# The same last stretch for one gated attention and Fourier kernel, with three reorderings in its first tenth: the third tokens' transposes behind scores, one copy behind the second keys' cast, the weights' exponential one tile later

## The chip, the cores and the metric

The kernel runs on one core of a Trainium2 chip. The core has five engines, each with its own in-order queue: PE (TensorE, matrix products, with weight loads shown as PEld), DVE (VectorE), ACT (ScalarE), POOL (GpSimd) and SP (SyncE, which here only issues DMAs; ACT and POOL issue some too). Engines meet through semaphores. The metric is the device time of one execution in microseconds; runs are compared by their medians, and the traces come from one profiled execution each.

## The reference

```python
def _A_ref(x, wqkv, wo):                      # x: 1 x 2048 x 448, 16 heads of 28
    qkv = (x @ wqkv).reshape(B, S, 3, H, Dh).transpose(2, 0, 3, 1, 4)
    q, k, v = qkv[0], qkv[1], qkv[2]
    scores = jnp.einsum("bhqd,bhkd->bhqk", q, k) * Dh ** -0.5
    p = softmax(scores, axis=-1)
    o = jnp.einsum("bhqk,bhkd->bhqd", p, v)
    return o.transpose(0, 2, 1, 3).reshape(B, S, D) @ wo

def _B_ref(x, w_r, w_i):
    X = rfft2(x.astype(float32), axes=(-2, -1)) * (w_r + 1j * w_i)
    return irfft2(X, s=(S, D), axes=(-2, -1)).astype(bfloat16)

g = sigmoid((x * gate_w).sum(-1, keepdims=True))
return g * _A_ref(x, A_wqkv, A_wo) + (1 - g) * _B_ref(x, B_w_r, B_w_i)
```

Only `A_x` is used as x in both halves. Inputs and the output are bfloat16.

## The kernel before

**Attention.** The 16 heads go in four groups T of four heads, and the 2048 queries in four chunks of 512, so there are 16 chunks c = 4T + qc. For one chunk there are 16 key blocks i of 128 keys and 4 heads h: 64 pieces of 128 keys by 512 queries. `score` (L824) makes one piece on PE with 32 rows of the array, so products of four heads can run side by side. Most pieces are gathered into tiles of three or two pieces in turn (`next_tile`, L1156): `scores` (L1001) writes the tile to a bank of PSUM, `exp` (L1067) runs ACT's exponential over it (L1077) into a tile Pt, and `pv` (L981) multiplies Pt by the values `vsb` into the accumulator psPV (L998). A part of the pieces is taken off ACT: `claim` hands a key block to `pack_step` (L837), which casts the scores on DVE (L843, tile Pd), and `chain` (L849) makes the exponential of it on DVE by seven steps. The values carry a column of ones (of weights `ek` for the first group), so psPV holds the softmax's sums too.

**Everything else** is cut into units of a few phases, each a few PE instructions followed by DVE work: transposes of x (`turn_unit`), projections of queries and keys (`first_unit` for the first group, `qk_unit` later), values (`v0_unit`, `v_unit`), the gate, the Fourier half as products with cosine and sine matrices (`f1_unit`, `a_unit`, `b_unit`, `i_unit`, `z_unit`), and the output tiles (`out_unit`, `base_unit`). They use two background banks of PSUM, bg0 and bg1, and in the beginning the accumulator's bank as a third (named pv).

**The order is written out when the program is built.** `stream` (L1330) walks over the tiles k with modelled clocks: `tp` for PE, `tv` for DVE, `ta` for ACT. For each tile it emits the exponential k, a few value products (`do_pv`, L1399), as many unit phases as fit (`pick`, `step` L1222), dummy products on a zero tile `warm` that keep PE busy (`zero`, `one_zero`, `until` at L1290 and L1296, `zeros` at L1034), and then the scores of tile k + 2, which use the PSUM bank that exponential k has read. Emission order is the order in each engine's queue; what it waits for follows from the tiles it touches. `bank_free` is the modelled time at which each of the three banks can be written again, and the bank that is free first takes the next unit.

**The head.** `head` (L299) brings the first 256-token pieces through by hand. Then the units in FIRSTS come: T1.2, T2.0, k0.1, T2.2, T3.0, k0.2, T3.2, k0.3, q0.1, ek0, W0 to W3. T2.0 and T2.2 are the two halves of the transposes of the third 512 tokens (448 columns of x in four pieces), each eight PE transposes (L296) and one DVE copy into xT (L447). k0.1 is the second 512 keys of the first group: two products and two more (L288), a DVE cast to `qraw` (L609) and its square `sqh` (L610), a product that adds the norms (L614), and the cast into kT (L618). The xtok tokens come by DMA from SP (L211, three loads of 512 tokens). The tiles' scores need kT of the block they read: the seventh tile is the first to use keys of k0.1. `ek_unit` finds each key's norm relative to the smallest one; its `weights` runs ACT's exponential (L488) and a DVE copy (L489) into vsb.

**The tail.** The last chunk's last four key blocks are cut in query parts of 256, 128 and 128 (`PARTS`, `split`), so that the end of one part is worked on while the next is computed. `pv_part` (L1456) multiplies the values of a part (L993), and when a part is complete DVE turns it (`over`: transposition L1555, reciprocal L1556, times gate L1557), scales it (`scaled`, L1560; on POOL for the first part, on DVE for the others) and turns it back into oT (`back`, L1565). `tail` (L1485) then makes output tiles 12 to 15. Each is what the earlier heads and the Fourier half gave (`base`, float32 in SBUF) plus the product of oT with Wo (`last_values`, L1543). For tiles 13 and 15 PE adds the base by a float32 product with the unit matrix (`sums`, L1538); for 14 DVE adds it (`add_base`, L820); for 12 ACT copies the product out (L1527) and POOL adds (L1528). The stores go out on SP's queue (12, 13, 14) and ACT's (15). Tile 12 and 13 use the first part, 14 the second, 15 the third.

Of the kernel before, what the change touches and what calls it, by code (L numbers as in the profile page):

```python
# [11 lines left out]
BF16 = mybir.dt.bfloat16  # L12
F16 = mybir.dt.float16
F32 = mybir.dt.float32
# [148 lines left out]
class Kernel:  # L163
# [286 lines left out]
    def ek_unit(self):  # L450
# [36 lines left out]
        def weights():  # L487
            nc.scalar.activation(out=ek[:], in_=ek[:], func=ACT.Exp, scale=-SCALE)  # L488
            nc.vector.tensor_copy(out=self.vsb[:, :, 0:4, DH], in_=ek[:].rearrange("p (t s) -> p t s", s=4))  # L489
            self.dve(0.25, at=self.ta + 0.4)  # L490
            self.marks["ek1"] = self.tp
# [489 lines left out]
    def pv(self, c, i, first, last):  # L981
        T = c // 4
        pcs = self.pieces.pop((c, i))
        self.packs -= self.pack_t[(c, i)] is not None
        if not isinstance(i, int):
            q0, w = PARTS[i[1]]
            n = len(i[2:])

            pairs = [(j, h) for j in range(n) for h in range(4)]
            if i[1] == len(PARTS) - 1:  # L990
                pairs.sort(key=lambda jh: jh[1])
            for j, h in pairs:
                self.nc.tensor.matmul(self.psPV[32 * h:32 * h + 32, q0:q0 + w], lhsT=self.vsb[:, i[2 + j], 4 * T + h, :],  # L993
                                      rhs=pcs[h][:, w * j:w * j + w], start=False, stop=True,
                                      tile_position=(0, 32 * h), skip_group_check=True)
# [71 lines left out]
    def exp(self, k):  # L1067
# [9 lines left out]
        self.nc.scalar.activation(out=Pt[:, 0:n, :], in_=ps[:, 0:n, :], func=ACT.Exp, scale=SCALE)  # L1077
        for e, (c, i, h) in enumerate(self.tiles[k]):
# [143 lines left out]
    def step(self, u, b, limit):  # L1222
# [15 lines left out]
        pe(ps)  # L1238
# [3 lines left out]
        if ve is not None:  # L1242
            self.dve(vcost, at=self.tp + PV)
            ve(ps)
            self.bank_free[b] = self.tv + VP
# [6 lines left out]
        return True  # L1252

# [76 lines left out]
    def stream(self):  # L1330
# [5 lines left out]
        self.ended, self.ot, self.held = False, None, None  # L1336
# [21 lines left out]
        while self.ring:  # L1358
# [34 lines left out]
            self.scores(k + 2, end)  # L1393
            self.fill_v(end - 0.2)
# [4 lines left out]
    def do_pv(self, k, left, most, limit=0.0):  # L1399
        done = 0  # L1400
        waited = False
        while done < most and self.pv_c < NC:
# [28 lines left out]
            if c == NC - 1 and (len(left[c]) == 1 or not isinstance(cand, int) and waited):  # L1431
                break
# [52 lines left out]
    def tail(self):  # L1485
# [8 lines left out]
        for i in sorted(left[c], key=lambda i: (i,) if isinstance(i, int) else i):  # L1494
            if len(left[c]) == 1:
# [15 lines left out]
                for e in (0, 1):  # L1511
                    self.last_values(pf[e], e, e == 0)
# [5 lines left out]
            else:  # L1518
                self.pv_part(i)
        for n in (3, 2) if self.N % 2 == 0 else (2, 3):  # L1520
            pf.append(self.psp.tile([P, n, QW], F32, name=f"ps{n}", tag=f"ps{n}", bufs=1)[:, 0])
# [12 lines left out]
        nc.scalar.dma_start(out=self.outv[:, 15, :], in_=fin[2][:, 0:D])  # L1534
# [87 lines left out]
```

## Time and profile before

| | us |
|---|---|
| median of 3 runs | 426.28 (426.26 to 426.36) |
| the profiled execution | 427.39 |
| its span, first to last instruction | 425.60 |
| granted TensorE clock, mean | 1.000 |
| ACT tile exponentials (L1077), main group | 385.3 in 339, mean 1.300 |
| PE score products (L829) | 143.7 in 926 |
| DVE casts Pd (L843) | 88.6 in 130 |
| PE value products (L998) | 79.9 in 818 |
| dummy products on PE (L1296 and L1034) | 40.1 in 124 and 35.3 in 92 |

A row of the timeline reads: start, time, engine, line, operation, output tile and inputs, shapes, how many; in brackets the idle time of the engine just before it and what ended that. Rows that follow each other with the same line are merged. A row of the waits names the waiting engine, line and tile, what it waited for, and the total, the number of times and the longest. Matmul ends are modelled, and a few records of matmuls are missing.

The chain that ended last gives PE 35% of the span, ACT 34%, DVE 19%, issue (time in which an engine waited for nothing that the profile shows) 9% and DMA 2%.

### The profile page before, as it was taken

How to read it: one execution, taken by the hardware profiler on the slowest of the kernel's cores; microseconds unless marked ns; L12 is line 12 of the kernel's file. 1: busy time of each engine (PE TensorE's matmuls, PEld its weight loads, DVE VectorE, ACT ScalarE, POOL GpSimd, SP SyncE). 2: the span in 40 equal slices, each digit the busy share in tenths (PEclk: the TensorE clock that was granted, in tenths of full speed). 3: DMA queues.
4: the chain of work that ended last, by engine and by line, in shares of the span. 5: the costliest groups of instructions: out<-in, count | busy, mean ns of one | idle time of the engine just before them, and what ended most of it. 6: DMA issues, size and time to landing. Idle time of an engine off the chain costs nothing.

```text
span 425.6 us, 8292 instructions
## 1 busy us (share of the span) xinstructions
PE 406.7 (96%) x3178; PEld 146.1 (34%) x3197; DVE 394.7 (93%) x650; ACT 411.9 (97%) x370; POOL 50.8 (12%) x57
## 2 busy tenths in 40 slices
PE   8999999999999999999999999999999999999995
PEld 5444233333333333333333333333343333333332
DVE  6569989999989999999999999999999999999994
ACT  4899999999999999999999999999999999999994
POOL 6000002020110111011220100202001011110101
PEclk9999999999999999999999999999999999999999
DMA  8900310422302153375664446536453305222132
GB/s 231 183 6 2 8 27 7 113 51 52 77 13 42 31 96 62 74 166 99 144 158 99 108 103 124 103 70 109 109 148 78 76 2 101 56 70 65 32 62 67
DMA packets 32404, 34.30 MB, mean 81 GB/s; under 512 B 14988, under 2 KB 25228, under 8 KB 32332
## 3 DMA queue, kind: packets, MB, share of 16 engines
q1 hardware_dynamic: 28012, 20.21, 20.7%
q0 software_dynamic: 3600, 13.11, 16.9%
q8 instruction: 25, 0.41, 0.4%
q10 hardware_dynamic: 752, 0.44, 0.4%
q14 instruction: 15, 0.12, 0.1%
HBM read 14.85 MB, written 1.95 MB: 39 GB/s over the span
## 4 chain that ended last, share of the span: by engine, by line
PE 35%; ACT 34%; DVE 19%; issue 9%; DMA 2%; SPq 0%; ACTq 0%; DVEq 0%
ACT Pt L1077 29%; PE psPV L998 7%; PE ps L829 6%; DVE Pd L843 4%; PE bg L829 3%; PE psPV L1296 3%; PE bg L288 3%; ACT early L1077 2%; PE bg L1034 2%; DMA xtok<-in_A_x_dram 2%; DVE pa L887 2%; DVE Pd L864 1%; DVE n L861 1%; DVE pa L873 1%; PE bg L673 1%
## 5 line engine op out<-in xcount | busy, mean ns | idle before, releaser
L1077 ACT ACTIVATE Pt<-ps 128x1024 bf16<-128x1024 f32 (+1 forms) x339 | 385.3, 1300 | 0.9 <-PE ps L829 0.4
L829 PE MATMUL ps<-qT,kT 32*128 32x512 bf16 (+2 forms) x926 | 143.7, 375 | 3.7 <-ACT Pt L1077 2.0
L843 DVE TENSOR_SCALAR Pd<-bg 128x512 uint16<-128x512 f32 x130 | 88.6, 682 | 4.8 <-PE ps L829 3.4
L998 PE MATMUL psPV<-Pt,vsb 128*32 128x512 bf16 x818 | 79.9, 388 | 0.0
L829 PEld LDWEIGHTS <-kT 32*128 32x128 bf16 x1056 | 45.7, 91 | 93.9 <-issue 88.9
L829 PE MATMUL bg<-qT,kT 32*128 32x512 bf16 x130 | 49.8, 383 | 0.8 <-DVE Pd L843 0.3
L890 POOL DMA_DIRECT2D Pd<-pa x25 | 24.0, 962 | 218.4 <-PE ps L829 110.6
L887 DVE TENSOR_TENSOR pa<-pa,n 128x2048 uint16<-128x2048 f16 (+2 forms) x33 | 40.4, 1225 | 0.6
L873 DVE TENSOR_TENSOR pa<-pa,n 128x2048 f16<-128x2048 f16 (+1 forms) x33 | 40.3, 1222 | 0.3
L998 PEld LDWEIGHTS <-vsb 128*32 128x32 bf16 x1008 | 23.1, 93 | 50.9 <-issue 50.2
L1296 PE MATMUL psPV<-warm 128*128 128x512 bf16 x124 | 40.1, 385 | 0.0
L1034 PE MATMUL bg<-warm 32*128 32x512 bf16 x92 | 35.3, 383 | 1.8 <-DVE Pd L843 1.4
L975 POOL TENSOR_TENSOR oT<-o,rep 128x512 bf16<-128x512 f32 x13 | 16.4, 1264 | 134.8 <-DVE oT L974 67.0
L288 PE MATMUL bg<-xT,Wg 128*128 128x512 bf16 (+1 forms) x93 | 28.1, 381 | 1.1
L864 DVE TENSOR_SCALAR Pd<-Pd 128x2048 uint16<-128x2048 uint16 (+1 forms) x33 | 24.0, 726 | 0.4
L861 DVE TENSOR_SCALAR n<-Pd 128x2048 uint16<-128x2048 uint16 (+1 forms) x33 | 22.6, 684 | 0.4
L876 DVE TENSOR_SCALAR pa<-pa 128x2048 f16<-128x2048 f16 (+1 forms) x33 | 22.8, 691 | 0.1
L869 DVE TENSOR_SCALAR pa<-n 128x2048 f16<-128x2048 uint16 (+1 forms) x33 | 22.2, 674 | 0.0
L684 DVE CAST U<-bg 128x450 bf16<-128x450 f32 x32 | 19.9, 621 | 2.0 <-PE bg L696 1.2
L1034 PEld LDWEIGHTS <-warm 32*128 32x128 bf16 x92 | 8.3, 91 | 29.0 <-issue 28.2
L1077 ACT ACTIVATE early<-ps 128x1024 bf16<-128x1024 f32 (+1 forms) x13 | 15.2, 1227 | 2.3 <-PE ps L829 2.3
L782 PE MATMUL bg<-Binv,VT 128*128 128x448 bf16 x64 | 16.5, 355 | 0.4 <-DVE fin L792 0.3
(190 smaller groups left out, 431.9 us busy)
## 6 DMA issues: line engine op xcount, KB each, us to landing
Pd<-pa POOLq DMA_DIRECT2D x25, 512.0 KB, 5.0
rep<-rD SPq DMA_DIRECT2D x52, 64.0 KB
CR<-cRB SPq DMA_DIRECT2D x8, 256.0 KB
UT<-U SPq DMA_DIRECT2D x16, 112.5 KB
VT<-U SPq DMA_DIRECT2D x16, 112.5 KB
CR<-cCS SPq DMA_DIRECT2D x8, 192.0 KB
xtok<-in_A_x_dram SPq DMA_DIRECT2D x3, 448.0 KB
out_dram<-fin SPq DMA_DIRECT2D x12, 112.0 KB
```

What stands on the lines that cost most here:

```text
L288: self.nc.tensor.matmul(ps[:], lhsT=self.Wg[T, q][0:k, c, :], rhs=self.xT[0:k, c, 512 * b:512 * b + 512], start=(c == 0), stop=(c == 3))
L829: self.nc.tensor.matmul(out[:, w * j:w * j + w], lhsT=self.kT[T][32 * h:32 * h + 32, 128 * i:128 * i + 128], rhs=self.qT[T][32 * h:32 * h ...
L843: nc.vector.tensor_scalar(out=pk["t"][:, h, :], in0=ps[:], scalar1=SCALE * LOG2E * 512.0, scalar2=127.0 * 512.0, op0=ALU.mult, op1=ALU.add)
L861: v.tensor_scalar(out=st["n"], in0=t, scalar1=511, scalar2=None, op0=ALU.bitwise_and)
L864: v.tensor_scalar(out=t, in0=t, scalar1=127 << 9, scalar2=2, op0=ALU.bitwise_and, op1=ALU.logical_shift_right)
L873: v.tensor_tensor(out=st["a"], in0=st["a"], in1=st["n"], op=ALU.mult)
L887: v.tensor_tensor(out=q, in0=st["a"], in1=st["n"], op=ALU.mult)
L890: nc.gpsimd.dma_start(out=t, in_=q, accum_op=ALU.add)
L998: self.nc.tensor.matmul(self.psPV[32 * h:32 * h + 32, :], lhsT=self.vsb[:, i, 4 * T + h, :], rhs=pcs[h], start=first, stop=last, tile_posi ...
L1034: self.nc.tensor.matmul(ps[:], lhsT=self.warm[sl], rhs=with_free(self.warm[sl], [[0, 4], [1, P]]), start=True, stop=True, tile_position=(3 ...
L1077: self.nc.scalar.activation(out=Pt[:, 0:n, :], in_=ps[:, 0:n, :], func=ACT.Exp, scale=SCALE)
L1296: self.nc.tensor.matmul(self.psPV[:], lhsT=self.warm[:], rhs=with_free(self.warm[:], [[0, 4], [1, P]]), start=False, stop=False, skip_grou ...
```

## The change

Three orders change in the first tenth. The transposes of T2.0 are held back (`behind`) and emitted after the scores that follow; the bank is taken as free 1.0 us later by the planner, and one dummy product in front of the next scores is no longer emitted. The DVE copy of T3.0 is held back (`held`) while unit k0.1 is open, and emitted behind k0.1's cast into kT; the two background banks exchange names from there on. The exponential of the weights and its copy (`next_exp`) are emitted behind the next tile's exponential instead of ahead of it.

In the last stretch, a part of the last chunk may be taken by `do_pv` although it was waited for, as long as the modelled time is not over the limit: eight of the sixteen 256-column value products move ahead of twelve score products. In the last part the products are ordered by key block over the heads 0 to 2, then the four of head 3 (which alone need the last exponential), instead of head by head. The products with Wo for tiles 12 and 13 move behind the last part's values. Tile 12 is added by DVE as tile 14 is, last of all, and its store comes last on SP's queue; ACT's copy and POOL's add for it are gone. No other order changes on any engine.

```diff
@@ ek_unit
         def weights():
-            nc.scalar.activation(out=ek[:], in_=ek[:], func=ACT.Exp, scale=-SCALE)
-            nc.vector.tensor_copy(out=self.vsb[:, :, 0:4, DH], in_=ek[:].rearrange("p (t s) -> p t s", s=4))
+            def emit():
+                nc.scalar.activation(out=ek[:], in_=ek[:], func=ACT.Exp, scale=-SCALE)
+                nc.vector.tensor_copy(out=self.vsb[:, :, 0:4, DH], in_=ek[:].rearrange("p (t s) -> p t s", s=4))
+
+            self.next_exp = emit
@@ pv
-            pairs = [(j, h) for j in range(n) for h in range(4)]
-            if i[1] == len(PARTS) - 1:
-                pairs.sort(key=lambda jh: jh[1])
-            for j, h in pairs:
-                self.nc.tensor.matmul(self.psPV[32 * h:32 * h + 32, q0:q0 + w], ...
+            def heads(hs):
+                for j, b in enumerate(i[2:]):
+                    for h in hs:
+                        self.nc.tensor.matmul(self.psPV[32 * h:32 * h + 32, q0:q0 + w], ...
+            if i[1] < len(PARTS) - 1:
+                heads(range(4))
+            else:
+                assert len(self.tiles[self.N - 1]) == 1
+                heads(range(3))
+                heads((3,))
@@ exp
         self.nc.scalar.activation(out=Pt[:, 0:n, :], in_=ps[:, 0:n, :], func=ACT.Exp, scale=SCALE)
+        if self.next_exp:
+            self.next_exp()
+            self.next_exp = None
@@ step
-        pe(ps)
+        more = 0.0
+        if u.name == "T2.0":
+            self.behind.append(lambda ve=ve: (pe(ps), ve(ps)))
+            ve, more = self.later, 1.0
+        else:
+            pe(ps)
...
-            ve(ps)
-            self.bank_free[b] = self.tv + VP
+            if u.name == "T3.0" and any(x.name == "k0.1" for x, _ in self.open.values()):
+                self.held = lambda: ve(ps)
+            else:
+                ve(ps)
+            self.bank_free[b] = self.tv + VP + more
+            if u.name == "k0.1" and not u.phases and self.held:
+                self.held()
+                self.held = None
+                self.bank_free[0:2] = self.bank_free[1] + 0.6, self.bank_free[0]
...
+    def later(self, ps):
+        pass
@@ stream
             self.scores(k + 2, end)
+            while self.behind:
+                self.behind.pop()()
@@ do_pv
-            if c == NC - 1 and (len(left[c]) == 1 or not isinstance(cand, int) and waited):
+            if c == NC - 1 and (len(left[c]) == 1 or not isinstance(cand, int) and waited and self.tp > limit):
@@ tail
                 self.sums(pf[1], 1)
-                for e in (0, 1):
-                    self.last_values(pf[e], e, e == 0)
...
                 self.pv_part(i)
+        for e in (0, 1):
+            self.last_values(pf[e], e, e == 0)
...
-        fin = [self.rot3.tile([P, F2], BF16, name="X1") for _ in range(3)]
-        half = self.rot2.tile([P, QW], F32, name="o32")
-        nc.scalar.copy(out=half[:, 0:D], in_=pf[0][:, 0:D])
-        nc.gpsimd.tensor_tensor(out=fin[0][:, 0:D], in0=half[:, 0:D], in1=self.base[12], op=ALU.add)
-        nc.sync.dma_start(out=self.outv[:, 12, :], in_=fin[0][:, 0:D])
-        nc.scalar.copy(out=fin[1][:, 0:D], in_=pf[1][:, 0:D])
-        nc.sync.dma_start(out=self.outv[:, 13, :], in_=fin[1][:, 0:D])
+        fin = [self.rot3.tile([P, F2], BF16, name="X1") for _ in range(2)]
+        nc.scalar.copy(out=fin[0][:, 0:D], in_=pf[1][:, 0:D])
+        nc.sync.dma_start(out=self.outv[:, 13, :], in_=fin[0][:, 0:D])
         self.add_base(pf[3], 14, nc.sync)
-        nc.scalar.copy(out=fin[2][:, 0:D], in_=pf[2][:, 0:D])
-        nc.scalar.dma_start(out=self.outv[:, 15, :], in_=fin[2][:, 0:D])
+        nc.scalar.copy(out=fin[1][:, 0:D], in_=pf[2][:, 0:D])
+        nc.scalar.dma_start(out=self.outv[:, 15, :], in_=fin[1][:, 0:D])
+        self.add_base(pf[0], 12, nc.sync)
```

More of the change, by code (lines that the diff above doesn't have):

```diff
@@ L986, in pv @@
             q0, w = PARTS[i[1]]
-            n = len(i[2:])
-            pairs = [(j, h) for j in range(n) for h in range(4)]
-            if i[1] == len(PARTS) - 1:
-                pairs.sort(key=lambda jh: jh[1])
-            for j, h in pairs:
-                self.nc.tensor.matmul(self.psPV[32 * h:32 * h + 32, q0:q0 + w], lhsT=self.vsb[:, i[2 + j], 4 * T + h, :],
-                                      rhs=pcs[h][:, w * j:w * j + w], start=False, stop=True,
-                                      tile_position=(0, 32 * h), skip_group_check=True)
+            def heads(hs):
+                for j, b in enumerate(i[2:]):
+                    for h in hs:
+                        self.nc.tensor.matmul(self.psPV[32 * h:32 * h + 32, q0:q0 + w], lhsT=self.vsb[:, b, 4 * T + h, :],
+                                              rhs=pcs[h][:, w * j:w * j + w], start=False, stop=True,
+                                              tile_position=(0, 32 * h), skip_group_check=True)
+            if i[1] < len(PARTS) - 1:
[4 more added lines that the diff above has]
+                heads((3,))
             return
@@ L1335, in stream @@
         self.dummies = self.owed = 0
-        self.ended, self.ot, self.held = False, None, None
+        self.ended, self.ot, self.held, self.next_exp = False, None, None, None
+        self.behind = []
         self.pv_c, self.pv_free, self.pv_open = 0, 0.0, False
```

## The prediction

> **What bounds the kernel now.** I read the page first: which engine is full.
>
> ```profile
> PE 406.7 (96%) x3178; PEld 146.1 (34%) x3197; DVE 394.7 (93%) x650; ACT 411.9 (97%) x370; POOL 50.8 (12%) x57
> ```
>
> ACT, which runs the exponentials, is busy 411.9 of 425.6 us. Second, who makes ACT wait, asked for 60 to 430 us (total, times, longest), and ACT's own rows in the head:
>
> ```profile
> ACT Pt L1077 <- PE ps L829: 0.4, 2, 0.2
> ```
>
> ```profile
> 9.05 2.36 ACT L1077 ACTIVATE early<-ps 128x1536 bf16<-128x1536 f32 x2 [0.71 <-PE ps L829]
> 12.55 4.65 ACT L1077 ACTIVATE early<-ps 128x1536 bf16<-128x1536 f32 x4 [1.14 <-PE ps L829]
> 17.67 1.45 ACT L1077 ACTIVATE early<-ps 128x1536 bf16<-128x1536 f32 x1 [0.47 <-PE ps L829]
> ```
>
> The reader is to see: from 17.67 us to the last exponential ACT loses 0.4 us to waits. What ACT gains before 17.67 therefore travels to the end, and what the tail gains behind the last exponential (418.30) comes on top. Two places matter. The first is PE in the head:
>
> ```profile
> 9.14 0.65 PE L296 MATMUL pv<-ident,xtok 128*112 128x128 bf16 x8
> 10.63 0.65 PE L296 MATMUL bg<-ident,xtok 128*112 128x128 bf16 x8 [0.83 <-DMA xtok<-in_A_x_dram]
> 11.77 0.38 PE L1290 MATMUL pv<-warm 128*128 128x512 bf16 x1
> 12.08 0.39 PE L829 MATMUL ps<-qT,kT 32*128 32x512 bf16 x3
> 17.24 0.39 PE L829 MATMUL ps<-qT,kT 32*128 32x512 bf16 x2 [0.21 <-DVE kT L618]
> ```
>
> The transposes of the third tokens stand ahead of the third tile's scores (12.08) and wait for a load until 10.63; ACT, free at 11.41, waits until 12.55. At 17.24 the seventh tile's scores wait for the second keys. Why these are late stands in DVE's rows, where the last copy is the one waited for:
>
> ```profile
> 14.96 0.42 DVE L610 TENSOR_TENSOR sqh<-qraw 128x512 bf16<-128x512 bf16 x1
> 15.30 0.68 DVE L447 COPY xT<-pv 112x1024 bf16<-112x1024 bf16 x1
> 15.90 0.68 DVE L447 COPY xT<-bg 112x1024 bf16<-112x1024 bf16 x1
> 16.50 0.68 DVE L618 CAST kT<-bg 128x512 bf16<-128x512 f32 x1
> ```
>
> Third, the tail, where the chain of waits runs PE, DVE, PE, DVE, PE, ACT:
>
> ```profile
> 415.95 0.62 PE L993 MATMUL psPV<-Pt,vsb 128*32 128x256 bf16 x16
> 417.13 0.41 PE L993 MATMUL psPV<-Pt,vsb 128*32 128x128 bf16 x16 [0.23 <-DVE ot L1555]
> 418.75 0.55 PE L1543 MATMUL bg<-Wo,oT 128*128 128x448 bf16 x2 [0.26 <-DVE oT L1565]
> 419.23 0.44 PE L993 MATMUL psPV<-Pt,vsb 128*32 128x128 bf16 x16
> 421.68 0.36 PE L1543 MATMUL ps<-Wo,oT 128*128 128x448 bf16 x1 [0.88 <-DVE oT L1565]
> ```
>
> ```profile
> 418.15 0.17 DVE L1557 TENSOR_TENSOR i<-i,g 128x4 f32<-128x4 f32 x1
> 419.76 0.32 DVE L1555 STREAM_TRANSPOSE ot<-psPV 128x128 f32<-128x128 f32 x1 [0.55 <-PE psPV L993]
> 420.33 0.62 DVE L1557 TENSOR_TENSOR i<-i,g 128x4 f32<-128x4 f32 x1
> ```
>
> ```profile
> 422.64 0.35 ACTq L1534 DMA_DIRECT2D out_dram<-X  x1
> ```
>
> The last values (419.23) stand in PE's queue behind two output products (418.75) that wait for DVE, though their last exponential ended at 418.30. The same small product on DVE (L1557) takes 0.17 once and 0.62 the second time; POOL's add for output tile 12 runs from 419.80 to 420.93, just over it.
>
> **The head, step by step.** New order on PE: transposes T1.2, three dummies, scores of the third tile, T2.0. The third dummy writes the bank that T1.2's copy leaves at 9.83+0.69 = 10.52, so it starts at 10.57. From that dummy to the exponential the trace has 12.55-11.77 = 0.78, hence 11.35; ACT is free at 11.31 (exponentials overlap by 0.10). Gain so far 1.20.
>
> PE goes on, with the trace's own distances: T2.0 0.32 behind the scores, 11.21 (the load landed at 10.59: 0.6 of cover; k0.1 and the fourth scores queue behind that wait); eight transposes 0.45; two products of k0.1 at 11.66 and 11.88; the fourth tile's scores 12.18 (the dummy ahead of them is gone); k0.1's other two 12.50 and 12.72; T2.2 12.95; the fifth tile's scores 13.49, whose exponential can start at 13.49+0.39+0.08 = 13.96. ACT would be free at 13.62 (11.35 plus 1.35 plus 0.92 for the two exponentials): a new wait of 0.34.
>
> DVE: the cast qraw starts 0.57 behind the last k0.1 product (as 14.16 to 13.59), 13.29; sqh 14.09 to 14.51; T2.2's copy 14.43 to 15.11. Now kT is next, not T3.0's copy: its norm product can run at 14.57 and is done by 14.99, so kT takes 15.03 to 15.71; the seventh scores start at 15.77, their exponential could at 16.23, and ACT comes free at 16.26. Trace: 17.67. **Gain in the head 1.41 us.** Check by idle times: 1.24 and 0.57 go (counted with the overlap), 0.40 are new.
>
> T3.0's copy follows, 15.63 to 16.31; the next instruction that needs it is PE's dummy at 16.61: hidden with 0.25 to spare. The keys k0.2 behind it are first needed by the thirteenth tile, over 3 us later than they are made. T2.0's copy on DVE runs at 11.9, where DVE stood idle for 2.15.
>
> The exponential of the weights (0.26 on ACT) is only exchanged with a tile's: ACT's sum stays. Its copy (0.31) falls behind a Pd cast that had 0.58 of idle ahead of it, and pushes the raw query by 0.31, of which 0.21 of idle ahead of W0's product takes most; the last 0.1 lies on DVE, which is not the bound. Without that cover it would cost 0.31 once. Price 0.
>
> Bounds for the head. Above: all idle goes, 1.81. Below: the landing records of the trace show fifteen of the sixteen parts of the third tokens' load in by 7.99 and one at 10.59; if that straggler comes early in an execution without profiler, the kernel before loses less. T2.0 would then run at 9.78, everything up to 12.55 would be 0.85 earlier, kT would end at 16.33 and the exponential start at 16.82: gain 0.56. I take 1.41, what this trace says.
>
> **The middle.** Between tail and head every engine's order is the same; the two background banks only change names. Nothing there hangs on absolute time but the initial loads, the last issued by 15.84. I carry the 1.41 through; bounds 0 and all of it.
>
> **The tail, in the old clock.** Eight of the sixteen 256-column value products move ahead of the twelve score products at 415.60, which wait for an exponential until 415.55; they take 0.22 of the 0.35 from 415.25 to 415.60, and the dummy there runs beside the scores. So the first part ends 0.22 earlier, and with it DVE's first transposition (416.41), the second part's values (416.91), and the float32 sums behind them (417.25 to 418.27). The last part's first twelve products start at 418.20, the four that need the last exponential (418.30) follow at 418.40 and are done by about 418.7. DVE is still at the second part until 419.00, so the last transposition starts at 419.03, not 419.76: 0.73.
> Then, 0.03 apart, 0.32, 0.18, 0.17 (POOL's add is gone, so L1557 costs 0.17, not 0.62: 0.46), 0.29, 0.31: oT complete at 420.40. PE meanwhile ran the two products for tiles 12 and 13 (0.58), the sums (0.86 to the next start), tile 14's product (to 420.35); tile 15's starts at 420.45, not 421.68; ACT copies at 420.86 and issues the store at 421.42, not 422.64. But tile 12 is new on DVE: add for 14 from 420.40, add for 12 (0.58 each, as L820) to 421.48, store 421.51. On SP's queue that store goes from first to last, so 13 and 14 no longer stand behind it. Both land 1.7 after issue as before (421.51 against 422.64): **gain in the tail 1.13 us.**
> Bounds: above 1.2 (tile 15's own path); below 0.6, if the last values end 0.4 later than I think, which tile 15's product then feels in full since PE has only 0.1 of slack there, and the stores of 12 and 15 get 0.15 in each other's way.
>
> The 0.46 rests on one overlap; POOL's product at 417.60 to 418.21 also touches an L1557 (418.15) and costs it nothing. If POOL is not the cause, the tail gives 0.67, within these bounds; I take 1.13, as the long row is the only one that lies under a POOL row from its start.
> [...]
>
> **Sum.** 1.41 + 1.13 = 2.54. Span 425.60 to 423.06; the profiled execution took 427.39, 1.79 more than its span, so it would take 424.85. The median of the runs shown, 426.28, is 1.11 below that execution; I take the same difference off it: **423.8 us**. Own range of this case 423.2 to 424.4.
>
> **Rivals.**
> 1. *The head pays little*: the straggler is the profiler's (for it: the profiled execution is 1.11 longer than the median; against it: nothing ties the 1.11 to that place), or DVE at 93% takes the shift up in mid-stream. 0.56 + 1.13: 424.6; nothing at all: 425.1.
> 2. *The tail gives it back*: the products now stacked behind the last values (0.58, 0.86, 0.35) or the second add decide. With no gain there 426.28-1.41 = 424.9. Against it: 1.1 us of lateness is needed, the stack's own slack is 0.1 but its rows are all measured.
> 3. *It does not do what it says*: kT is held up elsewhere (its norm product, its qraw) and the tail's POOL add was harmless: under 0.85 in all, 425.5 to 426.3.
> 4. *Slower: PE's clock drops in the head.* One dummy product is taken out and the order of full and partial ones changes. The windows row (busy times of PE, weight loads, DVE, ACT, POOL, then the granted clock) speaks against it:
>
> ```profile
> 9.00:10.60 1.60, 0.79 (x11) 0.51 (x8) 1.43 (x3) 1.55 (x2) 0.00 (x0) 1.00 1.11 139
> ```
>
> PE idles half of this stretch and the clock stays 1.00, there and in the stretches behind it; the new order idles less. If it fell to half: PE is busy 6.62 of the 7.10 us from 10.60 to 17.70, so each such microsecond costs 0.93. From 2.7 us on it eats the 2.54; 4 us of it give 427.5.
> [...]
>
> **How the numbers follow.** Forecast 0.62, rival 1 0.17, rival 2 0.10, rival 3 0.06, rival 4 0.05. A measurement of this kernel can tell about 0.2%, 0.85 us, from no change. Forecast, 1 and 2 are all faster by more: 0.89; rival 3 is within: 0.06; rival 4 slower: 0.05. Range: 2.54 with the lower bounds 0.56 and 0.6 gives 425.1; with the upper 1.81 and 1.2, 423.3; with 0.1 for the measurement 423.2 to 425.1.
>
> **What would show it.** The third exponential's wait (1.14) gone, a wait of about 0.3 before the fifth, the seventh starting near 16.3; POOL without its last add; L1557 at 0.17 three times; the last transposition 0.3 or less after the one before it; the last store from SP, not ACT, about 2.5 earlier. Wrong: ACT waits beyond 20 us, granted clock under 1.00, a tile 15 product that waits for PE and not for DVE.

## The result, and the profile after

| | before | after |
|---|---|---|
| median of 16 runs each, in turn on one chip | 426.53 us (426.19 to 428.20) | 425.28 us (424.90 to 426.50) |
| ratio | | 0.9966, 95% interval 0.9954 to 0.9977 |
| profiled execution / its span | 427.39 / 425.60 | 426.47 / 424.7 |
| granted TensorE clock in it | 1.000 | 0.995 |

The kernel is faster by 1.25 us at the median, where 2.5 were forecast, and 425.28 lies just above the range of 423.2 to 425.1. Before's own median is 426.53 in this series and not the 426.28 that the forecast starts from; as a gain, 1.25 lies at the lower end of the 1.2 to 3.1 that the range spans. Ratios here and below are taken over all runs of both kernels and are not those of the two medians. The profiled execution of after is one of the slowest of its sixteen, for a reason that its own trace shows below.

The sums of busy time hardly move (the page's first part: busy time, share, instructions):

```profile
PE 407.4 (96%) x3177; PEld 145.8 (34%) x3196; DVE 394.5 (93%) x651; ACT 411.6 (97%) x369; POOL 49.6 (12%) x56
```

POOL has lost its one add (50.8 to 49.6, 57 to 56); the rest is a matter of waits. The head first: the timeline of after, a group's start and time, engine, line, operation and tiles, in brackets the idle time ahead. The score products are now L832, the exponential L1084, the cast into kT L621.

```profile
8.96 4.67 ACT L1084 ACTIVATE early<-ps 128x1536 bf16<-128x1536 f32 x4 [0.69 <-PE ps L832]
13.92 3.72 ACT L1084 ACTIVATE early<-ps 128x1536 bf16<-128x1536 f32 x3 [0.29 <-PE ps L832]
...
10.80 0.39 PE L832 MATMUL ps<-qT,kT 32*128 32x512 bf16 x3
11.12 0.65 PE L296 MATMUL bg<-ident,xtok 128*112 128x128 bf16 x8
...
14.40 0.68 DVE L447 COPY xT<-pv 112x1024 bf16<-112x1024 bf16 x1
15.00 0.68 DVE L621 CAST kT<-bg 128x512 bf16<-128x512 f32 x1
15.60 0.68 DVE L447 COPY xT<-bg 112x1024 bf16<-112x1024 bf16 x1
```

The transposes of T2.0 (11.12) stand behind the third tile's scores (10.80), the cast into kT (15.00) ahead of T3.0's copy (15.60). ACT's wait of 1.14 ahead of the third exponential is gone, 0.29 ahead of the fifth is new, and the seventh starts at 16.19, the third of the second group.

So ACT is 1.48 us ahead of before at the seventh exponential. Of this, 0.09 was there at the first, which began at 8.96 instead of 9.05 and so before anything that the change moves; 1.39 is the change. ACT is still ahead by 1.45 at 276 us. At 306 us the lead is gone, though no order differs there. The waits of ACT (total, times, longest) and the windows show why (window, its length, then busy time and instructions of PE, weight loads, DVE, ACT and POOL, then the granted clock, DMA share and GB/s):

```profile
ACT Pt L1084 <- PE ps L832: 1.1, 4, 0.5
ACT Pt L1084 <- PE psPV L1005: 0.5, 1, 0.5
```

```profile
297.87:301.28 3.41, 3.11 (x19) 1.15 (x19) 3.34 (x7) 3.41 (x5) 1.05 (x1) 1.00 0.40 77
301.28:304.69 3.41, 3.41 (x22) 0.93 (x22) 3.39 (x5) 2.60 (x3) 0.00 (x0) 0.50 0.66 156
```

For 3.41 us PE ran at half clock. ACT was busy 2.60 of them instead of 3.41, and waited 1.1 us in all where before has 0.4 and no wait for psPV. That took the head's lead out of this one execution. A second profiled execution of the same kernel ("after, again" below) has no such stretch; its span is 423.3, so against the profiled execution of before the whole change is worth 2.3 us of span, where 2.54 were computed. Among the sixteen timed runs of after, three lie at 426.47 to 426.50 with a mean clock of 0.994 to 0.995; one of them is the execution with this stretch.

The tail, PE, DVE and the stores (L1570 the output products, L1582 to L1592 the turning, L1560 and L824 the stores of 15 and of 14 and 12):

```profile
418.19 0.54 PE L993 MATMUL psPV<-Pt,vsb 128*32 128x128 bf16 x16
418.66 0.55 PE L1570 MATMUL bg<-Wo,oT 128*128 128x448 bf16 x2
420.32 0.36 PE L1570 MATMUL ps<-Wo,oT 128*128 128x448 bf16 x1 [0.17 <-DVE oT L1592]
...
418.91 0.27 DVE L1582 STREAM_TRANSPOSE ot<-psPV 128x128 f32<-128x128 f32 x1
419.43 0.16 DVE L1584 TENSOR_TENSOR i<-i,g 128x4 f32<-128x4 f32 x1
...
421.29 0.38 ACTq L1560 DMA_DIRECT2D out_dram<-X  x1
420.85 0.86 SPq L824 DMA_DIRECT2D out_dram<-U  x2
```

The last values (418.19) stand ahead of the output products (418.66), the last transposition starts 0.85 earlier than before behind an exponential that ended at the same moment (418.30), the small product takes 0.16 instead of 0.62, and tile 15's store is issued at 421.29 instead of 422.64: 1.35 earlier. But the span ends only 0.93 earlier: by the landing records this store took 1.96 and tile 12's, issued 0.09 behind it at 421.38, took 2.04, where every one of before's four last stores took 1.66 to 1.71. Tile 12's is the one that lands last: it is issued 1.26 before the last store of before and gives 0.33 of that back.

### The profile page after: what moved, and what is told of

It reads as the page before. It is cut to its first block, busy times and chain, and to the rows that moved or that the text cites. A ratio compares the mean times of both kernels' runs of the same rounds, so it can differ in the third digit from the quotient of the medians.

```text
span 424.7 us, 8287 instructions
## 1 busy us (share of the span) xinstructions
PE 407.4 (96%) x3177; PEld 145.8 (34%) x3196; DVE 394.5 (93%) x651; ACT 411.6 (97%) x369; POOL 49.6 (12%) x56
## 4 chain that ended last, share of the span: by engine, by line
PE 40%; ACT 33%; DVE 16%; issue 9%; DVEq 0%; ACTq 0%
ACT Pt L1084 30%; PE psPV L1005 7%; PE ps L832 7%; PE bg L288 4%; PE bg L832 4%; PE psPV L1323 4%; DVE Pd L846 4%; ACT early L1084 2%; PE bg L1041 2%; DVE Pd L867 1%; DVE pa L890 1%; PE bg L676 1%; DVE n L864 1%; DVE U L687 1%; DVE pa L876 1%
## 5 line engine op out<-in xcount | busy, mean ns | idle before, releaser
L1084 ACT ACTIVATE Pt<-ps 128x1024 bf16<-128x1024 f32 (+1 forms) x339 | 385.8, 1301 | 2.1 <-PE ps L832 1.1
L832 PE MATMUL ps<-qT,kT 32*128 32x512 bf16 (+2 forms) x926 | 143.7, 376 | 3.6 <-ACT Pt L1084 2.0
L832 PEld LDWEIGHTS <-kT 32*128 32x128 bf16 x1056 | 45.6, 91 | 94.4 <-issue 89.4
L832 PE MATMUL bg<-qT,kT 32*128 32x512 bf16 x130 | 49.8, 383 | 0.8 <-DVE Pd L846 0.3
L1084 ACT ACTIVATE early<-ps 128x1024 bf16<-128x1024 f32 (+1 forms) x13 | 15.3, 1263 | 1.0 <-PE ps L832 1.0
```

The lines of the kernel that those rows point to most:

```text
L832: self.nc.tensor.matmul(out[:, w * j:w * j + w], lhsT=self.kT[T][32 * h:32 * h + 32, 128 * i:128 * i + 128], rhs=self.qT[T][32 * h:32 * h ...
```

## The experiments

All distances in this table come from the traces, one execution each; times from the first exponential's start (3rd, 7th: starts; last: end of the last exponential) or from the last exponential's end (span's end). "Full clock" is where the trace's first record of a full TensorE clock begins, "load" the last of the sixteen parts of the third tokens' load.

| kernel | full clock | first exp. | load | 3rd | 7th | last | span's end |
|---|---|---|---|---|---|---|---|
| before | 5.54 | 9.05 | 10.59 | 3.50 | 8.62 | 409.25 | 7.31 |
| before, again | 6.40 | 9.49 | 10.86 | 3.33 | 8.45 | 409.13 | 7.33 |
| tail only | 4.92 | 8.96 | 8.27 | 2.46 | 7.58 | 408.26 | 6.35 |
| POOL's add only | 6.61 | 9.53 | 8.80 | 2.46 | 7.58 | 408.26 | 7.39 |
| T2.0 only | 5.83 | 9.23 | 9.91 | 2.31 | 7.80 | 408.50 | 7.32 |
| T3.0's copy only | 6.26 | 9.39 | 7.92 | 2.46 | 7.01 | 407.73 | 7.33 |
| head only | 5.81 | 9.18 | 10.94 | 2.31 | 7.23 | 407.95 | 7.33 |
| after, again | 3.69 | 8.98 | 7.62 | 2.31 | 7.23 | 407.95 | 6.38 |
| after (half clock at 301 us) | 4.32 | 8.96 | 10.07 | 2.31 | 7.23 | 409.34 | 6.39 |
| after less T2.0's move | 6.21 | 9.39 | 8.82 | 2.46 | 7.01 | 407.81 | 6.40 |

### Head alone, tail alone, and both kernels again

Head only is after with the parts' values, `do_pv` and `tail` of before; tail only is after with `ek_unit` and `step` of before; the other two are unchanged. Of the edits against after, the lines that decide the order:

```diff
@@ do_pv
-            if c == NC - 1 and (len(left[c]) == 1 or not isinstance(cand, int) and waited and self.tp > limit):
+            if c == NC - 1 and (len(left[c]) == 1 or not isinstance(cand, int) and waited):
```

```diff
@@ weights
-            self.next_exp = emit
+            emit()
@@ step
-            self.behind.append(lambda ve=ve: (pe(ps), ve(ps)))
...
+        pe(ps)
...
-                self.held = lambda: ve(ps)
...
+            ve(ps)
```

> The three reorderings of the first tenth alone, with the last stretch of the kernel before. Theory A (the forecast's terms hold in every execution): 1.4 us faster than the kernel before, ratio 0.9967, and the seventh exponential starts near 16.2. Theory B (outside the one profiled execution the kernel before loses less in its head, so there is less to win): the trace looks the same, but the time is only 0.3 to 0.6 us below the kernel before, ratio 0.9986 to 0.9993.

> The last stretch alone, with the first tenth of the kernel before. Both theories: 0.9 us faster, ratio 0.998, as the two traces put the end of the changed one 0.93 us sooner behind the last exponential. If it is 0.3 or less, the tail and not the head is what the timed executions lack.

> The kernel before once more, unchanged, for a second trace. Theory A: a span near 425.6 with the seventh exponential at 17.7 whenever the clock is 1.00 throughout. Theory B: an execution of 426.3 us (span about 424.5) has its seventh exponential near 16.6 to 16.9, because the last part of the third tokens' load lands earlier than 10.6. A third possibility: the span's 1.1 us of difference lies somewhere else, behind 18 us.

> The changed kernel once more, unchanged, for a trace without the stretch at half clock near 301 us: without it ACT should be 1.4 to 1.5 us ahead of the kernel before at the last exponential, and the span 423.1 to 423.3. If the stretch comes back at the same place, it belongs to the change; if it is gone or elsewhere, it comes and goes.

Medians and ratios to the runs of before beside them (median 426.83, 426.29 to 430.62): head only 426.19, 0.9977 (0.9960 to 0.9994); tail only 425.92, 0.9979 (0.9967 to 0.9991); before again 426.85, 0.9994 (0.9983 to 1.0005); after again 425.31, 0.9959 (0.9944 to 0.9974). By the ratios each half is worth 0.9 to 1.0 us, and by the medians the head 0.64 and the tail 0.91. The interval of head only holds the ratios of Theory A and of Theory B, so it decides nothing between them. The ranges say more: head only spans 425.97 to 426.66, tail only 425.31 to 427.19. The fastest run of head only is 0.32 under the fastest of before, that of tail only 0.98. The tail takes time off every run; the head mainly cuts off the long ones.

The second trace of before fell on a long run again (427.82, load at 10.86, seventh exponential at 17.95) and so was no test of Theory B. After again is 1.37 us ahead of the profiled execution of before at the last exponential (1.4 to 1.5 expected), 0.07 of it from the first.

What tells the theories apart are ACT's rows of the tail-only kernel, whose head is that of before:

```profile
8.96 7.11 ACT L1084 ACTIVATE early<-ps 128x1536 bf16<-128x1536 f32 x6 [0.69 <-PE ps L832]
16.55 1.45 ACT L1084 ACTIVATE early<-ps 128x1536 bf16<-128x1536 f32 x1 [0.47 <-PE ps L832]
```

There is no wait of 1.14 between the second and the third exponential: they stand in one group. The third tokens' load was in at 8.27 here, not at 10.59, and the old order loses nothing to it. The seventh then starts at 16.55, 7.58 after the first, as Theory B has it (16.6 to 16.9); in before it was 8.62, in the new order it is 7.23 with a load at 7.62 and at 10.94 alike.

### T2.0 alone, T3.0's copy alone

Both are head only (with the weights' exponential as before), the first without `held`, the second without `behind`:

```diff
@@ step
-            if u.name == "T3.0" and any(x.name == "k0.1" for x, _ in self.open.values()):
-                self.held = lambda: ve(ps)
-            else:
-                ve(ps)
+            ve(ps)
```

```diff
@@ step
-        if u.name == "T2.0":
-            self.behind.append(lambda ve=ve: (pe(ps), ve(ps)))
-            ve, more = self.later, 1.0
-        else:
-            pe(ps)
+        pe(ps)
```

> Only T2.0's transposes are behind the scores; T3.0's copy, the weights' exponential and the whole tail are those of before. Theory B (the old head's time hangs on the last sixteenth of the third tokens' load, which came between 7.6 and 10.9 us so far): this edit alone takes that dependence away, so the runs at full granted clock lie within 0.8 us of each other, as those of the head-only kernel (425.97 to 426.66), and not over 1.5 us as those of before (426.3 to 427.9). The third exponential starts at 11.3 to 11.5 whatever the load does, the seventh at about 16.8 (T3.0's copy still stands ahead of kT: 0.6 later than the 16.2 to 16.4 of the full head). Median 426.2 to 426.6. Rival A (the spread of before comes from elsewhere, in mid-stream or the tail): the spread stays at 1.5 us or more.

> Only T3.0's copy is behind the cast into kT; T2.0 stands ahead of the scores as before, and the tail is that of before. Theory B: the third exponential follows the load (11.4 with a load at 8.3, 12.6 with one at 10.6), the seventh comes 0.6 earlier than in before at the same load (16.0 to 17.1), the runs keep a spread of 1.2 us or more, and the median lies 0.3 to 0.6 under that of before. Rival A: same spread as in the run with T2.0 alone. Rival C (the copy's place is worth nothing, kT waits for its norm product instead): seventh exponential as in before, ratio 1.000.

T2.0 alone: 427.04, ratio 1.0004 (0.9992 to 1.0015). T3.0's copy alone: 426.03, 0.9978 (0.9960 to 0.9996). The expected median of the first, 426.2 to 426.6, was missed. Its seventh exponential comes 7.80 after the first, which is what about 16.8 meant with a first at 9.05; it starts at 17.04 because the first is at 9.23. Against the old order with its load in time (7.58) 7.80 is 0.22 later, against the one with a late load (8.62) 0.82 earlier. The 0.22 comes from the new wait ahead of the fifth exponential (0.28 in this trace, 14.19 instead of 13.97), behind the transposes that now stand after the scores. The copy's place is worth 0.57 (7.58 to 7.01), near the 0.6 expected. In ACT's rows of that kernel the first seven exponentials follow each other with no wait over 0.1:

```profile
9.39 8.46 ACT L1080 ACTIVATE early<-ps 128x1536 bf16<-128x1536 f32 x7 [0.69 <-PE ps L832]
```

So the head is two edits of different kinds: the copy gave 0.57 wherever two traces with an early load, or two with T2.0's move, allow the comparison (7.58 to 7.01, 7.80 to 7.23); T2.0's move costs 0.22 and saves what a late load would take. The spreads agree, if less sharply than expected: 426.50 to 427.32 for T2.0 alone but for one run at 428.09 whose mean clock was 0.994; 425.63 to 427.10 for the copy alone (1.2 us or more expected).

### Tile 12's end: DVE or POOL

The first kernel is before with tile 12 added last by DVE; the second is after with ACT's copy and POOL's add; the third is the second with tile 12's store behind those of 13 and 14. Their edits in that order, each against the kernel it starts from:

```diff
@@ tail
-        half = self.rot2.tile([P, QW], F32, name="o32")
-        nc.scalar.copy(out=half[:, 0:D], in_=pf[0][:, 0:D])
-        nc.gpsimd.tensor_tensor(out=fin[0][:, 0:D], in0=half[:, 0:D], in1=self.base[12], op=ALU.add)
-        nc.sync.dma_start(out=self.outv[:, 12, :], in_=fin[0][:, 0:D])
...
+        self.add_base(pf[0], 12, nc.sync)
```

```diff
@@ tail
+        half = self.rot2.tile([P, QW], F32, name="o32")
+        nc.scalar.copy(out=half[:, 0:D], in_=pf[0][:, 0:D])
+        nc.gpsimd.tensor_tensor(out=fin[2][:, 0:D], in0=half[:, 0:D], in1=self.base[12], op=ALU.add)
+        nc.sync.dma_start(out=self.outv[:, 12, :], in_=fin[2][:, 0:D])
...
-        self.add_base(pf[0], 12, nc.sync)
```

```diff
@@ tail
-        nc.sync.dma_start(out=self.outv[:, 12, :], in_=fin[2][:, 0:D])
...
         self.add_base(pf[3], 14, nc.sync)
+        nc.sync.dma_start(out=self.outv[:, 12, :], in_=fin[2][:, 0:D])
```

> Before, with only tile 12's end changed: DVE adds it last of all and SP stores it last, instead of ACT's copy and POOL's add; the order of PE stays that of before. Theory (POOL's add is what stretched the third small product L1557 to 0.62): that row is 0.17, oT of the last part is complete 0.46 earlier against the last values, ACT issues tile 15's store 0.46 earlier, and the span ends 0.1 to 0.4 earlier, since tile 12's store comes last, next to tile 15's. Rival (the stretch has another cause, a wait for the gate or the reciprocal): the row stays at 0.6 and the end comes later by 0.1 to 0.3. Either way too small for the ratio: 0.999 to 1.001.

> After, with tile 12's end as in before: ACT copies its product out first, POOL adds, SP stores it first; DVE's second add is gone. All orders on PE stay those of after. If POOL's add stretches DVE's products of two SBUF inputs: the add begins at about 419.7, next to the last part's scaling (0.29 on DVE); that row or POOL's own is stretched by up to 0.9, tile 15's store is issued up to 0.9 later than in after, and the span is 0 to 0.9 longer. If POOL is harmless: the scaling stays at 0.29, tile 15's store is issued as in after and now lands alone, 1.7 after its issue instead of 1.96, and the span is about 0.3 shorter than that of after. Median 425.0 to 426.0.

> After, with tile 12 through ACT's copy and POOL's add, as in the run with that end, but its store emitted on SP behind those of 13 and 14. Against the last exponential's end the stores should then be issued at 2.0 (13), 2.55 (14), 2.99 (15, ACT's queue) and about 3.0 (12, when POOL is done at 2.61). If two stores issued within 0.1 us of each other each cost about 0.3 (1.96 and 2.04 in after, 1.67 alone), the last lands at about 5.0 and the span ends 0.1 earlier than in after, no more: distance from the last exponential's end to the span's end 6.3 against 6.40. Rival (the slow pair in after comes from the adds on DVE or from the queues, not from the nearness of the two): both land 1.7 after issue, 4.7, distance 6.0. Rival (POOL's add is stretched or stretches a product of DVE on some executions): distance 6.5 to 7. Median as after within 0.4.

POOL's add only: 426.82, ratio 1.0005 (0.9986 to 1.0024). The timeline, DVE and then the two last stores:

```profile
419.81 0.16 DVE L1554 TENSOR_TENSOR i<-i,g 128x4 f32<-128x4 f32 x1
...
421.66 0.38 ACTq L1530 DMA_DIRECT2D out_dram<-X  x1
421.18 0.86 SPq L821 DMA_DIRECT2D out_dram<-U  x2
```

The row is 0.16 instead of 0.62, so POOL's add was its cause. In before that add, which the row of 0.62 (from 420.33 to 420.95) overlaps, reads:

```profile
419.80 1.13 POOL L1528 TENSOR_TENSOR X<-o,late 128x448 bf16<-128x448 f32 x1 [1.59 <-ACT o L1527]
```

The row takes 0.62 or 0.63 in all six traces where this add runs beside it, and 0.16 in the eight others. In before it ends 0.02 behind the add (420.95 against 420.93). Through what the add holds it up, no run shows.

Tile 15's store is issued 3.88 behind the last exponential instead of 4.34, the 0.46 in full. Yet the span ends 7.39 behind it, not 7.31, where 0.1 to 0.4 less had been expected: tile 15's store took 2.17 and tile 12's, 0.04 later, 1.97. The gain was lost to two stores at one time.

After with POOL: 425.52, 0.9975 (0.9964 to 0.9985); span's end 6.74 behind the last exponential, 6.38 to 6.39 in after. Its stores on SP:

```profile
419.50 0.33 SPq L1559 DMA_DIRECT2D out_dram<-X  x1
419.93 0.38 SPq L1561 DMA_DIRECT2D out_dram<-X  x1
420.40 0.40 SPq L824 DMA_DIRECT2D out_dram<-U  x1
```

Tile 15's store goes out at 2.99 as in after, and no product of DVE is stretched (POOL's add runs from 418.29 and takes 1.19; the small product was done by 418.16, and the scaling, which had begun at 418.20, takes its 0.29). So neither of the two cases written came: what is late is SP's queue. Tile 12's store waits for POOL until 419.50, and 13's and 14's stand behind it, the last of them issued at 3.54. With the store of 12 emitted behind theirs: 425.33, 0.9966 (0.9954 to 0.9979), span's end 6.58. There 12 and 15 are issued together, at 2.98, and both take over 2 us (2.27 and 2.11):

```profile
419.87 0.37 ACTq L1564 DMA_DIRECT2D out_dram<-X  x1
419.86 0.38 SPq L1562 DMA_DIRECT2D out_dram<-X  x1
```

I had 6.3 for a collision and 6.0 without. The 6.58 also lies in the 6.5 to 7 of the third case, a stretched add, but the add is no cause here: it takes 1.18, the small product 0.16, and both stores go out when they were expected. The two adds on DVE are none either, since this kernel has only one. So two stores at one time are slower, and by more than was written; why they are is not shown. Both versions with POOL end later than after in the trace, by 0.35 and 0.2 us, too little for the ratios to tell.

### The load on another queue

```diff
         for b in range(1, 4):
-            nc.sync.dma_start(out=self.xtok[:, 4 * b:4 * b + 4, :], in_=xv[:, 4 * b:4 * b + 4, :])
+            (nc.scalar if b == 2 else nc.sync).dma_start(out=self.xtok[:, 4 * b:4 * b + 4, :], in_=xv[:, 4 * b:4 * b + 4, :])
```

> Before, with one edit: the load of the third tokens is issued on ACT's queue (the third one there) instead of as the second of three on SP's. All work on PE, DVE and POOL keeps its order. Theory B (what spreads the runs of before, 426.3 to 428.1, is the last sixteenth of this load, which holds T2.0 and with it the third tile's scores): issued about 0.9 earlier, the load's last part should land before 9.5; then the third exponential starts 2.5 after the first and the seventh 7.6 after it (as in the two executions with a load at 8.3 and 8.8), and the runs at full clock gather at 426.3 to 426.9 without those over 427.3, median 426.4. If the load's last part still lands past 10, the spread stays and the theory gets no test from the change of queue, only a further pair of numbers (load, distance of the exponentials). If it takes bandwidth from the second tokens' load, T1.0 and all behind it come later and the median rises by up to 1. Rival (the spread has another source): load early, spread as before.

429.46, ratio 1.0052 (1.0025 to 1.0078): slower. In the profiled execution the third tokens came at 8.52, but the last sixteenth of the second tokens, which went ahead of them before, came at 10.35, and everything stood behind it. PE's row, and the windows:

```profile
10.39 0.65 PE L296 MATMUL t<-ident,xtok 128*112 128x128 bf16 x8 [2.11 <-DMA xtok<-in_A_x_dram]
```

```profile
8.54:11.95 3.41, 1.56 (x20) 0.98 (x21) 0.96 (x3) 0.43 (x1) 0.00 (x0) 1.00 1.09 152
11.95:15.36 3.41, 3.34 (x21) 1.60 (x20) 1.65 (x3) 1.94 (x2) 0.00 (x0) 0.50 1.06 214
```

PE was busy 1.56 of 3.41 us in the first window, and the clock was 0.50 in the second. It is the expected third case, with the clock's drop on top and 2.7 us at the median where up to 1 was written. Three of the twelve runs lie at 426.56 to 426.62 and the other nine at 428.18 or over. It is no test of what spreads the runs of before, since another load was late in its place. That the late load causes those long runs therefore rests on the pairs of load and exponential in the table, and not on a run in which only the load was made early.

### The weights' exponential, and after without T2.0's move

The first is after with the weights' exponential at once, the second after with T2.0 as in the kernel with the copy alone:

```diff
@@ weights
-            self.next_exp = emit
+            emit()
```

> After, with the weights' exponential and its copy ahead of the next tile's exponential again, as in before. Price forecast: 0 (0.26 on ACT is only exchanged). So the distance from the first to the seventh exponential stays 7.23, that from the first to the last 407.9 to 408.0, the span 423.3 to 424, the median that of after within 0.2. Rival (the order matters: with the exponential ahead of the tile's, the next tile's start and all behind it are 0.26 later, or the values' weights come too early for a copy that holds DVE): the first-to-last distance grows by 0.1 to 0.3, which only the trace can tell.

> After, with T2.0's transposes ahead of the third tile's scores again, as in before; T3.0's copy behind the cast into kT, the weights' exponential and the tail as in after. Theory B: with the load in by about 9.3 this is faster than after: third exponential 2.46 after the first (after 2.31), fifth 4.74 (4.96), seventh 7.01 (7.23), last 407.73 (407.95), span's end 6.38 behind it, so the fastest runs lie at 424.7, 0.2 under those of after (424.9), and the median at 424.8 to 425.3; with the load at 10.6 or later it is slower than after, seventh about 8.0, and such runs lie at 425.4 to 426.1, so the range of the runs at full clock is 1 or more, where after has 0.7. Rival (T2.0's move is worth something whatever the load does, as the forecast's 1.41 had it): no run under 424.9 and the median 0.4 or more above that of after.

The exponential's place: 425.19, 0.9966 (0.9953 to 0.9978), the seventh 7.23 behind the first as in after. No effect, as forecast. Its trace has a half-clock stretch again, from 301.24, and a distance to the last exponential of 409.37, so that distance says nothing on the edit but repeats after's 409.34.

Without T2.0's move: 425.05 (424.88 to 426.11), 0.9956 (0.9942 to 0.9971), the best median of all. The distances are those expected (2.46, 4.74 and 7.01), but its fastest run lies at 424.88, not 424.7, and only one of nine is over 425.5. Against after's 425.28 and 425.31, from other series on other chips, nothing can be told from it: the move of T2.0 costs 0.22 in executions with an early load and guards against a late one, and how often a load is late decides. Of the first sixteen runs of before, six lie at 427.48 or over and the other ten at 426.91 or under.

## Why the prediction was half right

**The head's rows came out as computed.** Third exponential at 11.27 (computed 11.35), the fifth at 13.92 with a wait of 0.29 (0.34), kT from 15.00 (15.03), the seventh at 16.19 (16.26). All of them are 0.09 early because the first exponential is; taken from the first, the seventh comes at 7.23 where 7.21 was computed. Against the profiled execution of before that is a gain of 1.39, and 1.41 had been written. T3.0's copy is hidden, the weights' exponential cost nothing.

**The step that failed is the last one of the sum**: "it is 1.11 below that execution; I take the same difference off it". The 1.11 was taken as an offset common to both kernels. It was the very wait that the head's change takes away. The profiled execution had its load at 10.59 and its seventh exponential at 8.62 after the first; executions with a load by 8.8 have it at 7.58, 1.04 sooner, and the three runs that made the median of 426.28 fit those: first exponential at 9.05, 408.26 to the last one's end, 7.31 to the span's end and 1.79 beyond it make 426.41. No trace was taken of those three. So from that median the head could only give 7.58 - 7.23 = 0.35, of which 0.31 are left at the last exponential (408.26 to 407.95). Taking 1.41 off a median that lacked the late load counted the same microsecond twice.

**Rival 1 named this and priced it too high.** Its case is a load that comes early, and it holds, though not as an effect of the profiler: before's timed runs reach 428.2 too. Its price was 0.56. With an early load the third exponential of the old order starts 2.46 after the first, 1.04 sooner than in the profiled execution, where I had moved everything by 0.85; the new order is untouched. Hence 0.35. Most of the difference is one reading: I let T2.0 begin at 9.78, about where the eight transposes ahead of it end by the profile and 0.64 behind their start, and in the tail-only kernel it begins 0.49 behind it (9.06 and 9.55).

**The middle carries.** What the copy's place gives is 0.57 at the seventh exponential and 0.53 at the last; what T2.0's move costs is 0.22 and 0.24, and the whole head against a late load gives 1.39 and 1.30. The exception is the clock: 3.41 us at half speed near 301 us cost 409.34 - 407.95 = 1.39, or 0.41 for each microsecond; rival 4 had put the drop into the head at 0.93 each. Two of the signs of being wrong, waits of ACT beyond 20 us and a clock under 1.00, appeared in the profiled execution; after again has neither (clock 1.000, ACT's waits for scores 0.4 as in before), so both belong to that stretch.

**The tail gave 0.93 instead of 1.13.** The last transposition starts 0.85 earlier (0.73 computed), the small product's 0.46 came in full and its cause is confirmed, and tile 15's store is issued 1.35 earlier in its own time. The term that was mis-sized is the two stores in each other's way: nothing in the sum and up to 0.15 in its bound, an estimate that no trace shows, against a measured 0.3 for each (1.96 and 2.04 against 1.67 to 1.68 for the two ahead of them). Rival 2, that the stacked products or the second add eat the gain, doesn't hold: tile 15's product waits for DVE (0.17) and not for PE. The store behind the second add does land last, by 0.17 (423.42 against 423.25), but 0.93 of the gain is kept.

**The sum as it should have been**: 0.31 for the head with an early load and 0.93 for the tail make 1.24, off 426.28 gives 425.04. Measured: 424.90 for the fastest, 425.28 for the median. That 1.24 is so close to the 1.25 between the medians is luck in part, since each median holds late loads, half-clock stretches and late starts in its own share.

## What to carry to other kernels

Before a median and a profiled execution are set off against each other, find the place where the profiled one lost the difference; if the change touches that place, the gain may be counted twice. A reordering that takes work out from behind a load is worth what the load is late in a given execution (T2.0's move saves 0.82 at the seventh exponential against a load at 10.59 and costs 0.22 against one by 8.8): compare ranges, not only medians, and price it by the execution in which the load comes early. Where two stores were issued within 0.1 us of each other at the end of this kernel, each landed later than before's, which are issued 0.4 us or more apart (1.80 to 2.27 us against 1.66 to 1.71); keeping the last two apart is worth a try, but no run here shows an earlier end by it.

## What the runs showed that was not expected

**Where the clock's records begin.** In each trace the first record of a full TensorE clock begins between 3.48 and 6.61 us. The half-clock record of after near 301 us lasts 3.413 us and starts 301.28 - 4.32 = 296.96 behind the first full one, which is 87 times 3.413; with the late second tokens the distance is 11.95 - 5.12 = 6.83, which is twice. Until the first full clock PE's products follow each other about half as fast. Eight transposes of one line, which start 0.056 us apart in after (full clock from 4.32) and 0.107 us apart in after less T2.0's move (from 6.21):

```profile
5.16 0.65 PE L339 MATMUL tb<-ident,xtok 128*112 128x128 bf16 x8
```

```profile
5.34 1.03 PE L339 MATMUL tb<-ident,xtok 128*112 128x128 bf16 x8
```

The first exponential follows it: 8.88 to 8.98 in the six traces with a full clock before 5 us, then 9.05 (5.54), 9.18 (5.81), 9.23, 9.39, 9.39, 9.49 and 9.53 (6.61); the one kernel with a delayed load stands apart. So where the full clock begins shifts the start of the exponentials by up to 0.6 us from one execution to another.

**What stands ahead of a half clock.** In the 3.41 us ahead of the stretch at 301.28 PE was busy 3.11, and 1.56 in those ahead of the one with the late load. Other stretches of 3.41 us that begin a whole number of them behind the first full clock have PE busy less than 3.11, and the full clock stays behind them: 2.68 from 335.41 in after, 2.52 from 8.95 in before. So PE's busy time just ahead does not tell the two kinds apart. Both executions of this order of work in which such a 3.41 us begins at 301.24 to 301.28 have the half clock there; the three others of the whole new kernel or its variants with the same first exponential (full clock from 3.48 to 3.70) have none. In no trace of the old order does one begin nearer than 0.2 us to that place of the stream of exponentials, so whether the new order brings the half clock, or that place alone, is open. What sets it off is not shown.
